# A planner that orders TensorE's work, single-bank PSUM tiles and merged loads in an attention-and-gate kernel

## The chip, the cores and the metric

The kernel runs on one core of one Trainium2 chip. The metric is the device time of one execution in microseconds (us). The kernel before takes 529.25 us, the median of 5 runs (528.02 to 530.52). Engines are named as in the profile: PE is TensorE (its weight loads are PEld), DVE is VectorE, ACT is ScalarE, POOL is GpSimd, SP is SyncE.

One more quantity is used throughout: **us of columns**. A matmul streams its columns; 512 of them start 215 ns apart when the clock is full. Counted from the shapes in the trace, all matmuls of the kernel stream 327 us of columns at full clock (at 215 ns for 512 columns it would be 330 us; all counts here are that 1% low). That is the least time that TensorE could need, and the change does not touch it. A few matmul records can be missing from a trace; the sum found is 314 us for the kernel before. By the weight loads that have no matmul beside them, about 4 us of what is missing lie before 220 us in the kernel before, and about 3 us in the changed kernel.

## The reference, cut to what matters

```python
def attention(q, k, v, w_phi):            # 8 batches, 8 heads, 576 rows, 64 wide
    def phi(x):
        proj = x @ w_phi                   # 64 -> 128 features
        proj = proj - max(abs(proj), axis=-1)
        return concat([exp(proj), exp(-proj)], axis=-1)
    qp, kp = phi(q), phi(k)
    kv, z = kp^T @ v, sum(kp, rows)
    return (qp @ kv) / (qp @ z + 1e-6)

def gate(x, w_proj, filter_fft, w_out):    # x: 8 x 576 x 512
    x1, x2, x3 = split(x @ w_proj, 3)
    conv = irfft(rfft(x2) * rfft(filter_fft))
    return (x1 * conv * x3) @ w_out

out = gate(attention(...))
```

The work falls into 16 attention units (one for half the heads of a batch) and 8 gate batches. A gate batch needs both attention units of its batch: the attention output is transposed (`xT`), folded on POOL (`G`), multiplied by the weights (`x2`), transformed (`fwd`), multiplied by the filter's spectrum (`spec`), transformed back (`inv`) and multiplied by the output weights (`fin`). The filter's spectrum and the trig tables for the transforms are computed once at the start; this is called the set-up here.

## The kernel before

First, steps are put in a fixed order by time numbers:

```python
TIMES = [0.00, 0.03, 0.06, 0.10, 0.16, 0.22, ...]       # the 18 steps of a unit
for t in range(NHALF):                                  # 16 attention units
    if t >= 2:
        order.append((t - 1.5, ld))                     # its loads
    for i in range(18):
        order.append((t + TIMES[i], run))
for b in range(NB):                                     # 8 gate batches
    for i, fn in enumerate(gs):
        order.append((2 * b + 2.2 + 2.0 * i / len(gs), fn))
order.sort(key=lambda x: x[0])
```

So one gate batch is spread over the two attention units that come after its own. Attention and gate run in lockstep.

Second, the projections go through two PSUM tiles of two banks each, and one reduce or exponential reads a whole tile:

```python
def proj(c, shape, name):
    return c.psum.tile(shape, FP32, name=name, tag="proj", bufs=2)

def pk(hp):
    pp = proj(c, [P, 2, 4, P], "Pk")
    # ... 4 matmuls of 256 columns ...
    nc.vector.tensor_reduce(out=mxk..., in_=pp, op=ALU.max, apply_absolute_value=True)
    nc.scalar.activation(s.Ekp[hp], pp, AF.Exp, scale=1.0)
    nc.scalar.activation(s.Ekm[hp], pp, AF.Exp, scale=-1.0)
    # the row maxima go into v: exp(-+max), then v times it, on POOL
    nc.gpsimd.tensor_tensor(out=v12[:, sg, :, 0:HD], in0=s.vs[...], in1=v12[:, sg, :, 64:65]..., op=ALU.mult)
```

Third, each unit issues 12 loads on POOL's queue (24 a batch); `q` comes in four pieces. Fourth, two small VectorE steps make the transposed maxima of `q`, and the output transpose is copied out in one contiguous copy:

```python
def mt():
    nc.vector.tensor_copy(M2[:, :, :, 0], mxq)
    nc.vector.tensor_tensor(out=M2[:, :, :, 1], in0=mxq, in1=M2[:, :, :, 0], op=ALU.subtract)
    # ... 5 transposes, copy to mT ...
```

## Time and profile before

| kernel before | value |
|---|---|
| time | 529.25 us (528.02 to 530.52) |
| PE busy | 387.4 us, 73% |
| POOL busy | 325.4 us, 62% |
| DVE busy | 297.9 us, 56% |
| ACT busy | 243.1 us, 46% |
| columns to stream | 327 us |

The first lines of the page of the kernel before: busy time per engine, then the busy tenths of two engines and of the granted TensorE clock in 40 equal slices of 13.2 us, then the engines of the chain that ended last.

```profile
PE 387.4 (73%) x3600; PEld 227.0 (43%) x3661; DVE 297.9 (56%) x512; ACT 243.1 (46%) x451; POOL 325.4 (62%) x454
...
PE   1134627696878779787878778877978698878796
...
POOL 9949996949566592759385674659294534344400
PEclk9999859798998999799989999799979989989999
...
POOL 39%; PE 20%; issue 18%; ACT 10%; DVE 9%; DMA 3%; POOLq 0%; DVEq 0%; ACTq 0%
```

No engine is full over the span. PE runs mostly at seven or eight tenths from a quarter of the way on; POOL is nearly full in the first quarter.

The waits view of the kernel before: the engine that stood idle and its instruction, what ended the wait, then the total in us, how often, and the longest.

```profile
POOL ks L349 <- PE ktp L375: 76.6, 11, 8.9
...
POOL v L409 <- ACT v L404: 29.2, 10, 4.1
...
PE acc L596 <- POOL G L242: 26.0, 8, 4.1
```

POOL stands 76.6 us at loads that wait for a buffer, and TensorE then waits 26.0 us for the fold `G` that POOL does late.

The windows view of the kernel before: busy us of each engine (and instructions) in four stretches, the mean clock, the DMA share and GB/s.

```profile
0.00:100.00 100.00, 39.26 (x373) 27.09 (x378) 60.84 (x132) 34.45 (x67) 88.11 (x132) 0.89 0.74 79
100.00:220.00 120.00, 97.52 (x896) 56.23 (x910) 66.44 (x106) 58.73 (x108) 79.50 (x110) 0.91 0.40 50
220.00:340.00 120.00, 97.16 (x908) 56.11 (x924) 67.08 (x111) 60.12 (x110) 76.32 (x106) 0.94 0.40 50
340.00:460.00 120.00, 98.27 (x966) 57.88 (x982) 66.30 (x108) 64.81 (x122) 65.16 (x89) 0.96 0.26 38
```

The first number after the length is PE, the third DVE, the fourth ACT, the fifth POOL. After 100 us the kernel is in a steady state: PE busy 97 of 120 us in every stretch.

Three groups of instructions of the kernel before (line, engine, operation, out<-in and shapes, count, busy us and mean ns of one, idle before it):

```profile
L409 POOL TENSOR_TENSOR v<-vs,v 128x512 bf16<-128x512 bf16 x64 | 66.2, 1061 | 29.3 <-ACT v L404 29.2
...
L427 DVE TENSOR_REDUCE mxk<-Pk 128x8 f32<-128x1024 f32 x32 | 38.9, 1217 | 8.1 <-PE Pk L421 7.9
L430 ACT ACTIVATE Ekp<-Pk 128x1024 bf16<-128x1024 f32 x32 | 32.8, 1024 | 19.3 <-DVE mxk L427 19.3
```

### The profile page before, as it was taken

Reading aid. Unit: us, or ns where it says so; the run is one execution under the profiler, and the core shown is the slowest. Engines: PE = TensorE matmul, PEld = TensorE weight load, DVE = VectorE, ACT = ScalarE, POOL = GpSimd, SP = SyncE. Lnnn points to the kernel's source line nnn. Section 1 sums busy time; section 2 is a strip of 40 time slices with the busy share of each in tenths; the row PEclk is TensorE's granted clock in tenths of the full one; section 3 lists DMA queues with packets and bytes.
Section 4 is the critical chain, followed back from the end, with each engine's and each line's share of the span. In section 5 each row is a group of like instructions: output and inputs, shape, how many; then the busy total and the mean of one; then the engine's idle time right before and its main releaser. Section 6 shows DMA issues by size and latency. Waiting matters only on the chain.

```text
span 527.5 us, 9126 instructions
## 1 busy us (share of the span) xinstructions
PE 387.4 (73%) x3600; PEld 227.0 (43%) x3661; DVE 297.9 (56%) x512; ACT 243.1 (46%) x451; POOL 325.4 (62%) x454
## 2 busy tenths in 40 slices
PE   1134627696878779787878778877978698878796
PEld 1023515253544546344544535344635455454443
DVE  2980774429462767439452947258551947385353
ACT  0345225383526552474337453466238443835240
POOL 9949996949566592759385674659294534344400
PEclk9999859798998999799989999799979989989999
DMA  7998615525261713525272525243372002000202
GB/s 70 84 202 77 56 18 52 45 24 47 24 127 9 66 22 66 73 24 46 24 134 25 46 24 110 27 47 23 64 94 25 0 1 91 1 1 1 90 1 90
DMA packets 71882, 27.03 MB, mean 51 GB/s; under 512 B 49120, under 2 KB 66720, under 8 KB 71840
## 3 DMA queue, kind: packets, MB, share of 16 engines
q0 software_dynamic: 66432, 16.89, 34.0%
q1 hardware_dynamic: 5408, 9.57, 5.0%
q8 instruction: 28, 0.46, 0.4%
q14 instruction: 14, 0.11, 0.1%
HBM read 33.75 MB, written 9.44 MB: 82 GB/s over the span
## 4 chain that ended last, share of the span: by engine, by line
POOL 39%; PE 20%; issue 18%; ACT 10%; DVE 9%; DMA 3%; POOLq 0%; DVEq 0%; ACTq 0%
POOL v L409 6%; PE acc L596 5%; POOL qs L353 5%; POOL vt L471 3%; PE acc L623 3%; POOL eox L237 3%; POOL kt L344 3%; POOL eox L238 3%; POOL G L242 3%; POOL G L243 3%; ACT Eqm L505 3%; DMA wproj<-in_moe_w_proj_dram 2%; POOL vt L344 2%; ACT Eqp L500 2%; DVE P L615 2%
## 5 line engine op out<-in xcount | busy, mean ns | idle before, releaser
L409 POOL TENSOR_TENSOR v<-vs,v 128x512 bf16<-128x512 bf16 x64 | 66.2, 1061 | 29.3 <-ACT v L404 29.2
L623 PE MATMUL acc<-xT,wproj 128*128 128x64 bf16 (+1 forms) x496 | 75.9, 289 | 0.5
L596 PE MATMUL acc<-wproj,G 128*128 128x512 bf16 x126 | 45.2, 487 | 27.3 <-POOL G L242 26.0
L349 POOL DMA_DIRECT2D ks<-in_k_dram x16 | 12.5, 781 | 78.0 <-PE ktp L375 76.6
L441 DVE TENSOR_REDUCE mxq<-Qn 128x8 f32<-128x1024 f32 x32 | 38.9, 1216 | 32.5 <-PE Qn L439 32.5
L353 POOL DMA_DIRECT2D qs<-in_q_dram x64 | 48.8, 785 | 4.0 <-PE xtp L557 2.7
L598 ACT CAST x2n<-acc 128x512 bf16<-128x512 f32 x40 | 23.5, 589 | 51.1 <-PE acc L596 46.2
L674 DVE TENSOR_TENSOR yT<-acc,ts 128x512 bf16<-128x512 f32 x32 | 22.2, 692 | 43.2 <-PE acc L664 43.2
L500 ACT ACTIVATE Eqp<-Pq 128x1024 bf16<-128x1024 f32 x32 | 33.2, 1037 | 27.6 <-PE Pq L495 23.6
L505 ACT ACTIVATE Eqm<-Pq 128x1024 bf16<-128x1024 f32 x32 | 32.7, 1022 | 23.5 <-PE Pq L502 21.5
L427 DVE TENSOR_REDUCE mxk<-Pk 128x8 f32<-128x1024 f32 x32 | 38.9, 1217 | 8.1 <-PE Pk L421 7.9
L430 ACT ACTIVATE Ekp<-Pk 128x1024 bf16<-128x1024 f32 x32 | 32.8, 1024 | 19.3 <-DVE mxk L427 19.3
L543 DVE RECIPROCAL r<-NE 128x10 f32<-128x10 f32 x32 | 6.9, 216 | 61.4 <-PE NE L539 61.4
L664 PE MATMUL acc<-IV,Y 128*128 128x512 bf16 (+1 forms) x254 | 41.2, 285 | 0.4
L623 PEld LDWEIGHTS <-wproj 128*128 128x128 bf16 x512 | 32.6, 99 | 17.5 <-issue 1.7
L690 PE MATMUL acc<-wout,yT 128*128 128x512 bf16 x147 | 39.5, 379 | 0.7
L633 ACT CAST x1s<-acc 128x512 bf16<-128x512 f32 x32 | 18.9, 590 | 44.2 <-PE acc L623 40.7
L439 PE MATMUL Qn<-wpp,qT 128*128 128x256 bf16 x128 | 22.9, 310 | 19.3 <-DVE qT L391 16.5
L596 PEld LDWEIGHTS <-G 128*128 128x128 bf16 x128 | 13.5, 116 | 50.0 <-POOL G L242 29.8
L694 ACT COPY o<-acc 128x512 f32<-128x512 f32 x16 | 9.4, 586 | 53.9 <-PE acc L690 41.3
L569 POOL COPY xT<-xT 128x2 bf16<-128x2 bf16 x16 | 3.5, 221 | 47.8 <-DVE xT L567 47.8
L431 ACT ACTIVATE Ekm<-Pk 128x1024 bf16<-128x1024 f32 x32 | 32.8, 1025 | 0.0
(180 smaller groups left out, 1091.9 us busy)
## 6 DMA issues: line engine op xcount, KB each, us to landing
out_dram<-o SPq DMA_DIRECT2D x32, 256.0 KB, 2.2
ks<-in_k_dram POOLq DMA_DIRECT2D x16, 256.0 KB, 4.4
qs<-in_q_dram POOLq DMA_DIRECT2D x64, 64.0 KB, 3.4
vs<-in_v_dram POOLq DMA_DIRECT2D x16, 256.0 KB, 4.2
wproj<-in_moe_w_proj_dram POOLq DMA_DIRECT2D x4, 384.0 KB, 10.0
out_dram<-o SPq DMA_DIRECT2D x8, 128.0 KB, 3.0
kt<-in_k_dram POOLq DMA_DIRECT2D x32, 16.0 KB, 3.4
qt<-in_q_dram POOLq DMA_DIRECT2D x32, 16.0 KB, 2.2
```

The costliest lines, as they stand in the source:

```text
L353: nc.gpsimd.dma_start(out=s.qs[:, ci, :, :], in_=q[b, h0:h0 + 4, ci * P:(ci + 1) * P, :].rearrange("h p d -> p h d"))
L409: nc.gpsimd.tensor_tensor(out=v12[:, sg, :, 0:HD], in0=s.vs[:, 2 * hp:2 * hp + 2, :, :].rearrange("p j c d -> p (j c) d"), in1=v12[:, sg, ...
L427: nc.vector.tensor_reduce(out=s.mxk[:, 8 * hp:8 * hp + 8].rearrange("p (j c) -> p j c", j=2), in_=pp, axis=AX.X, op=ALU.max, apply_absolut ...
L430: nc.scalar.activation(s.Ekp[hp], pp, AF.Exp, bias=0.0, scale=1.0)
L431: nc.scalar.activation(s.Ekm[hp], pp, AF.Exp, bias=0.0, scale=-1.0)
L441: nc.vector.tensor_reduce(out=mxq[:, 0:4, 2 * hp:2 * hp + 2], in_=pp, axis=AX.X, op=ALU.max, apply_absolute_value=True)
L500: nc.scalar.activation(s.Eqp[hp], pp, AF.Exp, bias=0.0, scale=1.0)
L505: nc.scalar.activation(s.Eqm[hp], pp, AF.Exp, bias=0.0, scale=-1.0)
L596: nc.tensor.matmul(acc, lhsT=lhsT, rhs=c.wproj[:, kt, 512:1024], start=(kt == 0), stop=(kt == 3))
L623: nc.tensor.matmul(acc, lhsT=c.wproj[:, kt, base + m * P:base + (m + 1) * P], rhs=xT[:, kt, s0:s1], start=(kt == 0), stop=(kt == 3))
L664: nc.tensor.matmul(acc, lhsT=Y, rhs=c.IV[:, kt, s0:s1], start=(kt == 0), stop=(kt == 5))
L690: nc.tensor.matmul(acc, lhsT=yT[:, kt, ci * P:(ci + 1) * P], rhs=c.wout[:, kt, :], start=(kt == 0), stop=(kt == 3))
```

## The change

The intent is to keep TensorE fed. The fixed time numbers go; every step becomes an object with its TensorE time, its needs and the engine work that it causes, and a planner simulates the engines while the kernel is being built. It takes, at each point, the first step that can start without delay, attention before gate. Attention thereby runs ahead of the gate, and gate steps fill TensorE's holes. Alongside: the two-bank PSUM tiles become single banks, with a reduce and two exponentials for each; loads are merged into 11 issues a batch; `spec` is cut in four and the tails in two; `xT` is written in another row order, by a strided copy of 512 columns and a short one.

```diff
-TIMES = [0.00, 0.03, 0.06, 0.10, 0.16, 0.22, ...]
+class Planner:
+    # free time of each engine, events, PSUM slots
+    def run(self, streams, window):
+        while any(streams):
+            best = None
+            for r, strm in enumerate(streams):
+                for k, st in enumerate(strm[:window(r)]):
+                    t = self.start_of(st)
+                    late = max(0, t - self.free["PE"] - 40)
+                    if best is None or late < best[0]:
+                        best = (late, strm, k)
+                    ...                       # stop at the first with late == 0
+            st = best[1].pop(best[2]); self.emit(st); out.append(st)

-def proj(c, shape, name):
-    return c.psum.tile(shape, FP32, name=name, tag="proj", bufs=2)
+def halves(c, shape, name):
+    return [c.psum.tile(shape, FP32, name=name, tag="proj", bufs=4) for _ in range(2)]

-            nc.scalar.activation(s.Ekp[hp], pp, AF.Exp, bias=0.0, scale=1.0)
+            for (i, j) in enumerate((1, 0)):
+                nc.vector.tensor_reduce(out=mx[:, 4 * i:4 * i + 4], in_=pp[i], ...)
+                nc.scalar.activation(Ep[:, j], pp[j], AF.Exp, bias=0.0, scale=1.0)
+                nc.scalar.activation(Em[:, j], pp[j], AF.Exp, bias=0.0, scale=-1.0)

-    s.ks = c.stage.tile([P, 4, 4, HD], BF16, name="ks", tag="ks", bufs=3)
+            setattr(s, nm, c.stage.tile([P, 2, 4, 4, HD], BF16, name=nm, tag=nm, bufs=2))
 ...
-            nc.vector.tensor_copy(xT[:, kt, 0:SEQ], tp[:, 0:SEQ])
+            nc.vector.tensor_copy(xTs[b][:, kt, 0:512].rearrange("d (p c) -> d p c", c=4),
+                                  tp[:, 0:512].rearrange("d (c p) -> d p c", c=4))
+            nc.vector.tensor_copy(xTs[b][:, kt, 512:SEQ], tp[:, 512:SEQ])
 ...
-    for _, fn in order:
-        fn()
+    pl.free.update({"PE": 8000, "ACT": 14000, "DVE": 14000, "POOL": 8000, "DMA": 8000})
+    order = pl.run([loads, attn, gate], (1, 26, 12).__getitem__)
+    for st in order:
+        st.fn()
```

## The prediction

> **What bounds it now.** No engine is full. In each steady batch (58.1 us from one batch's first x2 matmul to the next, 158.3 to 390.7 us, windows view) PE is busy 46.7 us, POOL 37.9, DVE 32.6, ACT 28.8. The matmuls stream 327 us of columns at full clock in all (counted from the shapes; 40.3 us a batch; a 512-column matmul starts every 215 ns). The rest is order: POOL stands about 8.9 us a batch at a k load that waits for the k transposes (77 us in all, waits view), issues 24 loads a batch (16.8 us), and only then folds; PE waits 3.6-4.1 us a batch for G from the fold (26 us). After that wait the granted clock is 0.50-0.56 for some 6 us (425 ns per 512 columns), about 3 us lost a batch. The Trainium skill ("TensorE: Matmul & The Clock Gate", Part 1) describes just this halving after an idle window; the trace agrees. The start is worse: the first x2 matmul begins at 100.9 us; POOL is nearly full until there, PE at 20-60%.
>
> **What changes.** (1) A planner orders all steps so that PE always has something ready; attention runs ahead of the gate. In the built order the last attention matmul comes after about 220 us of the 327 us of columns; the last 107 are pure gate. (2) PSUM tiles of two banks become single banks. (3) Loads per batch: 24 issues become 11; q in 1 KB runs. (4) spec is cut in four, tails in two.
>
> **Cost by engine, from durations in the trace.**
> - POOL a batch: folds 11 + v 8.5 + vt 3.3 + issues 11 x 0.75 = 31, less overlap 4% = 30 us (was 38). All eight, with 10 us of spectrum folds and 15 us of set-up and weight issues: about 263 us.
> - DVE: a 512 reduce, interpolated between 415 ns (256) and 1217 ns (1024), is 0.68 us; 64 more of each kind add 9.5 us each. Smaller xn steps add 11. The xT copy becomes strided: 0.44 us contiguous becomes about 0.8 us in two pieces (I take the uncompressed rate of the 683 ns 512 copy): +11. In all 298 to about 335.
> - ACT: 1024 exps of 1.02 us become two of 0.60: +20; ten table loads of 1.28 us at the start instead of two: +10; in all about 285.
> - PE: the same columns.
>
> **Sum.** Phase A, until attention ends: POOL 263, DVE 257, ACT 241, PE 235 us. All close, so none will be filled: plus 12 us of start and 15 of friction, about 290 us. Phase B: 107 us of gate, which keeps PE near full (at 500-520 us PE is busy 19.9 of 20 at clock 1.00): about 115. End: 5. Together about 412 us.
>
> **Predicted 412 us**, 388 to 450; faster by over 2% 0.97, within 0.02, slower 0.01.
>
> **Right if the profile shows:** POOL total 255-275 us busy, DVE 320-350, ACT 270-300; PE share over 80%; first x2 at 80-92 us; PE windows after about 295 us at 9 tenths with clock near 1.0 and POOL empty; half-clock stretches after G waits gone; POOL's wait for k transposes below 25 us; packets down from 66,432 by about 25,000. In phase A the chain of waits runs over POOL, ACT and DVE.
>
> **Wrong if:** in-order queues block each other in phase A (ACT behind table loads, POOL behind a load whose buffer isn't free), pushing it above 320 us; or the start's load queue holds attention of batch 0 up; or bubbles between spec, inv and fin in phase B exceed 4 us a batch. Better than said if phase A's engines reach 95%.

## The result, and the profile after

The changed kernel takes 457.3 us (median of 9 runs, 455.76 to 458.88), the kernel before 529.93 us in the same rounds (median of 16). The ratio is 0.8632, with a 95% interval of 0.8615 to 0.8648. A ratio here is the mean time of one kernel's fast runs over the mean time of the other's fast runs of the same rounds, so it is not quite the ratio of the medians that are quoted. Executions over 1.5% slower than the fastest of the same kernel are left out of the means. The kernel is faster by 14%, about 45 us less than the predicted gain, and outside the predicted range of 388 to 450 us.

The same lines of the page of the changed kernel (40 slices of 11.4 us).

```profile
PE 378.7 (83%) x3679; PEld 236.3 (52%) x3725; DVE 329.8 (73%) x703; ACT 261.5 (58%) x604; POOL 265.3 (58%) x352
...
PE   3326877579688769799798989999999999999995
...
POOL 9946998979966996954964647164542345000000
PEclk9659868698899969989899999999999999999999
...
PE 45%; POOL 20%; DVE 14%; ACT 8%; issue 8%; DMA 4%; DVEq 0%; POOLq 0%; ACTq 0%
```

PE's row has two halves. In the first 16 slices (some 180 us) it hardly differs from the kernel before: mostly five to eight tenths, with the clock dropping again and again. From the 23rd slice on (some 250 us) it stands at eight or nine tenths, mostly nine, with the clock at full.

The waits view of the changed kernel:

```profile
POOL v L608 <- ACT v L604: 30.3, 9, 5.1
...
POOL ks L499 <- PE kTp L560: 4.6, 3, 2.7
...
PE KV L722 <- POOL v L608: 14.2, 10, 4.9
PE Pk L589 <- DVE mxq L625: 10.0, 9, 5.0
```

POOL's wait for the `k` buffers fell from 76.6 to 4.6 us, and TensorE's 26.0 us wait for the fold `G` is gone from the list. What TensorE waits for now is `v` from POOL and the row maxima from DVE.

The windows view of the changed kernel, in the same stretches as before:

```profile
0.00:100.00 100.00, 58.09 (x595) 41.16 (x598) 71.45 (x192) 62.22 (x136) 84.87 (x126) 0.80 0.75 95
100.00:220.00 120.00, 98.95 (x1162) 68.77 (x1173) 95.76 (x207) 81.89 (x208) 95.52 (x126) 0.93 0.52 66
220.00:340.00 120.00, 113.46 (x1192) 72.39 (x1208) 100.62 (x205) 78.72 (x193) 66.35 (x83) 0.99 0.15 31
340.00:460.00 120.00, 108.24 (x735) 53.94 (x748) 61.99 (x103) 38.71 (x71) 18.54 (x19) 0.99 0.15 50
```

Between 100 and 220 us PE is busy 98.95 us, against 97.52 before: nothing gained, although DVE went from 66 to 96 us and ACT from 59 to 82. From 220 us on PE is busy 113 of 120 us, and POOL only 66. (The last stretch ends with the span at 454.6 us.)

Busy time hides half clock, so the columns that were streamed say it better. This table is counted from the matmuls in the traces:

| us of columns streamed by | 100 us | 220 us | 340 us | last attention matmul (`NE`) |
|---|---|---|---|---|
| kernel before | 23 | 102 | 182 | 491 us |
| changed kernel | 34 | 112 | 214 | 342 us |

By 220 us the change has brought only 10 us of columns (9 with the missing records put back, 115 against 106). All the rest of its 72 us comes later, when attention is ahead and the gate work that has piled up keeps TensorE full.

The groups of the changed kernel that answer to those shown of before:

```profile
L608 POOL TENSOR_TENSOR v<-vs,v 128x512 bf16<-128x512 bf16 x64 | 69.1, 1109 | 30.4 <-ACT v L604 30.3
...
L598 DVE TENSOR_REDUCE mxk<-Pk 128x4 f32<-128x512 f32 x64 | 42.3, 680 | 7.5 <-PE Pk L589 4.6
L602 ACT ACTIVATE Ekm<-Pk 128x512 bf16<-128x512 f32 x64 | 39.9, 626 | 0.0
```

The reduce of half the size takes 680 ns, as the prediction had interpolated; two of them cost more than one of 1217 ns.

### The profile page after: what moved, and what is told of

It reads as the page before. It is cut to its first block, busy times and chain, and to the rows that moved or that the text cites. A ratio compares the mean times of both kernels' runs of the same rounds, so it can differ in the third digit from the quotient of the medians.

```text
span 454.6 us, 9516 instructions
## 1 busy us (share of the span) xinstructions
PE 378.7 (83%) x3679; PEld 236.3 (52%) x3725; DVE 329.8 (73%) x703; ACT 261.5 (58%) x604; POOL 265.3 (58%) x352
## 3 DMA queue, kind: packets, MB, share of 16 engines
q0 software_dynamic: 40256, 16.88, 31.3%
## 4 chain that ended last, share of the span: by engine, by line
PE 45%; POOL 20%; DVE 14%; ACT 8%; issue 8%; DMA 4%; DVEq 0%; POOLq 0%; ACTq 0%
PE acc L931 10%; PE acc L972 8%; POOL v L608 6%; PE acc L896 5%; PE acc L998 5%; PE NE L745 3%; POOL vt L672 3%; DVE mxq L625 2%; DMA out_dram<-o 2%; DMA vt<-in_v_dram 2%; POOL vt L494 2%; ACT Eqp L697 2%; DVE mxk L598 1%; ACT Eqm L709 1%; PE KV L722 1%
## 5 line engine op out<-in xcount | busy, mean ns | idle before, releaser
L697 ACT ACTIVATE Eqp<-Pq 128x512 bf16<-128x512 f32 x64 | 36.4, 628 | 40.3 <-PE Pq L691 40.0
L601 ACT ACTIVATE Ekp<-Pk 128x512 bf16<-128x512 f32 x64 | 39.5, 622 | 31.9 <-PE Pk L589 28.0
L598 DVE TENSOR_REDUCE mxk<-Pk 128x4 f32<-128x512 f32 x64 | 42.3, 680 | 7.5 <-PE Pk L589 4.6
L625 DVE TENSOR_REDUCE mxq<-Qn 128x4 f32<-128x512 f32 x64 | 40.9, 680 | 2.2 <-PE Qn L621 2.2
L602 ACT ACTIVATE Ekm<-Pk 128x512 bf16<-128x512 f32 x64 | 39.9, 626 | 0.0
L709 ACT ACTIVATE Eqm<-Pq 128x512 bf16<-128x512 f32 x64 | 36.7, 648 | 2.8 <-PE Pq L706 2.6
L589 PE MATMUL Pk<-wpp,kT 128*128 128x256 bf16 x128 | 23.8, 292 | 13.8 <-DVE mxq L625 10.0
L722 PE MATMUL KV<-v,Ekp 128*128 128x65 bf16 x256 | 21.1, 208 | 11.9 <-POOL v L608 11.7
L672 POOL TENSOR_TENSOR vt<-vt,emt 128x130 bf16<-128x130 bf16 x64 | 23.9, 401 | 11.4 <-ACT emt L668 11.4
L751 DVE TENSOR_TENSOR xn<-NE,rc 128x320 bf16<-128x320 f32 x64 | 29.0, 483 | 0.3
## 6 DMA issues: line engine op xcount, KB each, us to landing
wproj<-in_moe_w_proj_dram POOLq DMA_DIRECT2D x4, 384.0 KB, 10.6
```

The lines of the kernel that those rows point to most:

```text
L598: nc.vector.tensor_reduce(out=mx[:, 4 * i:4 * i + 4], in_=pp[i], axis=AX.X, op=ALU.max, apply_absolute_value=True)
L601: nc.scalar.activation(Ep[:, j], pp[j], AF.Exp, bias=0.0, scale=1.0)
L602: nc.scalar.activation(Em[:, j], pp[j], AF.Exp, bias=0.0, scale=-1.0)
L625: nc.vector.tensor_reduce(out=mxq[:, 0:4, 2 * hp + j], in_=pp[j], axis=AX.X, op=ALU.max, apply_absolute_value=True)
L672: nc.gpsimd.tensor_tensor(out=s.vt12[:, sg, hp], in0=sg_of().vt[:, g, hp], in1=emt[:, sg].to_broadcast([P, 2, 65]), op=ALU.mult)
L697: nc.scalar.activation(s.Eqp[hp][:, j].rearrange("f (c p) -> f c p", c=4), pp[j], AF.Exp, bias=0.0, scale=1.0)
```

## The experiments

Eighteen kernels were run, each against the kernel before on the same chip. The texts call the theories by letters. The first two were A, that POOL's throughput bounds the first half, and S, that a late start does. Later ones were Q (POOL's load queue at the start), C (TensorE's half clock), M (what the planner doesn't know becomes a stall that is never made up), D (VectorE), O (the order holds gate work back) and P (set-up work fills the first 100 us). Differences "against the changed kernel" are between medians and its 457.3 us. All diffs are against the changed kernel and cut to what matters. The columns of ww_late come from a slow run.

| run | median us | ratio to before, 95% interval | columns by 100 / 220 / 340 us |
|---|---|---|---|
| (changed kernel) | 457.3 | 0.8632 (0.8615 to 0.8648) | 34 / 112 / 214 |
| old_order | 531.5 | 1.0026 (1.0004 to 1.0047) | 30 / 111 / 192 |
| psum_pair | 490.4 | 0.9240 (0.9208 to 0.9273) | 31 / 97 / 190 |
| split_loads | 456.4 | 0.8622 (0.8563 to 0.8680) | 34 / 118 / 223 |
| dup_early | 475.6 | 0.8985 (0.8965 to 0.9005) | 32 / 101 / 203 |
| dup_late | 468.2 | 0.8846 (0.8822 to 0.8869) | 35 / 113 / 210 |
| dup_early_told | 470.0 | 0.8839 (0.8803 to 0.8875) | 34 / 111 / 208 |
| ffold_dve | 458.4 | 0.8658 (0.8633 to 0.8683) | 35 / 115 / 219 |
| trig_first | 459.9 | 0.8688 (0.8662 to 0.8713) | 33 / 113 / 216 |
| ww_late | 470.4 | 0.8803 (0.8753 to 0.8852) | 33 / 103 / 203 |
| start_late | 470.8 | 0.8899 (0.8867 to 0.8930) | 28 / 103 / 207 |
| plan_cal | 459.0 | 0.8648 (0.8631 to 0.8665) | 35 / 116 / 219 |
| warm | 467.1 | 0.8795 (0.8765 to 0.8825) | 34 / 106 / 209 (without the dummies) |
| mx_act | 454.4 | 0.8547 (0.8520 to 0.8573) | 34 / 115 / 218 |
| dve_light | 451.0 | 0.8509 (0.8482 to 0.8536) | 33 / 118 / 227 |
| start_light | 454.5 | 0.8578 (0.8530 to 0.8625) | 33 / 113 / 223 |
| gate_first | 494.2 | 0.9325 (0.9295 to 0.9355) | 34 / 125 / 214 |
| no_setup (wrong result) | 449.3 | 0.8491 (0.8466 to 0.8515) | 40 / 115 / 214 |
| no_setup_start (wrong result) | 440.1 | 0.8308 (0.8292 to 0.8323) | 43 / 116 / 222 |

### Which part of the change brings the gain

**old_order**: every other part of the change, but the old kernel's fixed times in place of the planner.

```diff
-    order = pl.run([loads, attn, gate], (1, 26, 12).__getitem__)
+    timed = [(old time of the step, st) for st in loads + attn + gate]   # units at t, gate at 2b+2.2...
+    order = [st for _, st in sorted(timed, key=lambda x: x[0])]
```

> All parts of the change but the planner: the new steps (loads per batch, single PSUM banks, cut spec and tails) in the old kernel's fixed time order. If the order is the main gain, 495 to 525 us; if the smaller loads and tiles are, 455 to 480 us.

It took 531.5 us, as long as the kernel before, and longer than either expectation. Without the planner the other parts together bring nothing. One by one, only the single banks (psum_pair) and the merged loads (split_loads) were tried; the cut `spec` and tails and the new row order of `xT` were not.

**psum_pair**: the planner, but the projections in two PSUM tiles of two banks again. Each half is still read by its own instruction; only the release is by pair.

```diff
-    return [c.psum.tile(shape, FP32, name=name, tag="proj", bufs=4) for _ in range(2)]
+    t = c.psum.tile([P, 2, 512], FP32, name=name, tag="proj", bufs=2)
+    return [t[:, j, :]... for j in range(2)]
```

> The changed kernel with the four single PSUM banks put back into two tiles of two banks. The planner counts pairs anyway, so the plan is the same. If finer PSUM tiles matter: 465 to 480; if not: 455 to 461.

It took 490.4 us, 33 us more, and more than the text had expected. So with the planner up to 33 of the 72 us hang on the single banks; old_order has them too and gains nothing. Not all of the 33 us need be owed to the release by pair. In the kept trace the two steps on `M` got stuck at 41 us, beside `v` and `vt` products of POOL, for 7.7 and 3.3 us, and the first `KV` came at 54.4 us instead of 41.9; what this is worth was not measured.

**split_loads**: 18 load issues a batch instead of 11 for batches 1 to 7; the planner knows of them.

```diff
-    halves = [(0, 1), (1, 2)] if b == 0 else [(0, 2)]
+    halves = [(0, 1), (1, 2)]
```

> The changed kernel with 18 load issues a batch instead of 11 for batches 1 to 7: 7 x 7 x 0.65 = 32 us more POOL work, about 23 us of it before 200 us. By the slope that the doubled v work showed (about 1 early, 0.6 late): 20 to 30 us longer, 477 to 487. If only work between the k max and KV counts and the issues fall into idle time: under 8 us longer.

It took 456.4 us: no change. The windows view of split_loads and then of the changed kernel, from 60 to 220 us:

```profile
60.00:220.00 160.00, 125.65 (x1399) 82.96 (x1396) 126.53 (x260) 104.20 (x257) 154.73 (x208) 0.91 0.51 62
```

```profile
60.00:220.00 160.00, 128.21 (x1472) 90.44 (x1488) 123.36 (x267) 102.38 (x258) 132.00 (x178) 0.90 0.56 69
```

POOL is busy 154.73 of 160 us instead of 132.00, and the kernel is as fast. An engine that can take 23 us more in the very stretch that loses the time is not what limits it by its throughput. Theory A falls in this form, and the merged loads, by themselves, bring nothing here. One rival is left: the smaller loads may also have helped attention by landing piece by piece, and this run does not separate the two. The chain of waits says where POOL still counts. From 42 to 220 us, 89 of its 178 us lie on POOL in the changed kernel, and 48 in split_loads, where DVE has 68; from 220 to 340 us none of it lies on POOL in either, and PE leads with 71 and 63 us.

### POOL's work on the way to KV

**dup_early** and **dup_late** do the `v` products of head pair 0 twice, in units 0 to 7 or in units 8 to 15; the second overwrites the first with the same values. The planner isn't told.

```diff
-            for sg in range(2):
+            for sg in ((0, 1, 0, 1) if hp == 0 and t < 8 else (0, 1)):      # dup_late: t >= 8
                 nc.gpsimd.tensor_tensor(out=v12[:, sg, :, 0:HD]...
```

> The changed kernel with the two v multiplications of the first head pair done twice in units 0 to 7 (same values again): 8 x 2 x 1.06 = 17 us more work on POOL, all of it in about the first 190 us. Theory A (the first 200 us are paced by POOL, busy 175 of 200 us there, the rest by PE): 10 to 17 us longer than the changed kernel, so 467 to 474. Rival B (the time is lost to PE's order and half clock, POOL is only a neighbour): under 5 us longer. Rival C (PE paces everything): no change.

> The same doubling in units 8 to 15 instead: again 17 us more on POOL, but nearly all after 180 us, where POOL idles half the time and PE is 94 to 99% busy. Theory A: 0 to 3 us longer (457 to 460). If POOL paced the attention to its end, as the prediction had it: 10 us or more longer.

dup_early added some 17 us of POOL work (15.8 by the busy time) and cost 18.3 us, a little more than theory A's 10 to 17. dup_late cost 10.9 us, where theory A had expected almost nothing: most of the loss falls at 220 to 240 us, before the piled-up gate work keeps TensorE full (PE is busy 11.2 us there, 17.3 in the changed kernel). In the same 20 us two steps on `M` took 2.2 and 3.8 us in dup_late, so a part of the cost may be what VectorE loses beside POOL (see ffold_dve below) and not the length of the chain.

**dup_early_told** is dup_early with the planner's cost for these products doubled as well.

```diff
-                  ("POOL", pool(512), ("em" + h,), "v1_" + h),
+                  ("POOL", pool(512) * (2 if hp == 0 and t < 8 else 1), ("em" + h,), "v1_" + h),
```

> The same 17 us of extra GpSimd work as in dup_early (v products of head pair 0 twice in units 0 to 7), but the planner's own cost for them is doubled too, so it can order around them. Its plan then ends 3.9 us later than the changed kernel's plan. Theory M (what the plan doesn't know becomes a TensorE stall, one for one, that is never made up; what it knows it can hide): 458 to 464 us, so most of dup_early's 18.3 us come back. Rival theory A (GpSimd's throughput in the first half is the bound): 472 to 478 us, as dup_early.

It took 470.0 us, between the two expectations: knowing the cost brings back 6 of the 18 us by the medians (8 by the ratios). Theory M is right in a small part only. Read with split_loads, these runs suggest that it matters where POOL's work stands: 23 us of load issues off the chain cost nothing, and 17 us on the chain from the row maxima through `v` to `KV` cost 11 to 18.

**ffold_dve** takes the filter's fold (10.6 us) off POOL and gives it to DVE.

```diff
-            fold(c, nc.gpsimd, st["fT"], st["G"], kt, 2, "f")
+            fold(c, nc.vector, st["fT"], st["G"], kt, 2, "f")
```

> The changed kernel with the fold of the filter spectrum on DVE instead of POOL: 10.6 us of POOL work between 50 and 61 us go away and some 6 us of DVE work come. Theory A: 6 to 10 us shorter (447 to 451). Rival B: under 3 us.

It took 458.4 us: no gain. One of the moved steps met the `v` products. The tile view of ffold_dve, with durations in ns as shortest, median and longest:

```profile
L371 DVE TENSOR_TENSOR Gf<-eof x2: 458/4698/8937, 40.6 to 51.7; 128x580 bf16<-128x580 bf16 x2
```

The same step took 0.46 us once and 8.94 us the other time, while POOL ran 14 `v` and `vt` products back to back. So this run says little about POOL's load; it shows what DVE loses beside POOL.

### The start

The first `KV` matmul comes at 41.9 us. POOL issues loads until 40.8 us, held up from 22.6 us on, and ACT's exponentials for the tails wait behind trig table loads until 34.6 us. The next runs take these holds away.

**trig_first** computes the trig tables ahead of everything (table loads fall from 11 to 4).

```diff
+    for g in trig_groups(c):
+        g()
     make_consts(c, w_phi)
 ...
-    for g in trig_groups(c):
-        g()
```

> The changed kernel with the trigonometric tables emitted before the constants and loads: the built order then has 4 activation table loads instead of 11 at the start. Theory S (the start is late by ACT's table switching and DVE's table arithmetic; the changed kernel's first KV ends at 47 us): 7 to 12 us shorter. Theory A in its strict form (POOL, held at the load queue to 40.8 us by the weights' landing, paces the start too): under 3 us shorter.

459.9 us: no gain. The trace shows that POOL's first `v` product still starts at 41.9 us.

**ww_late** loads the gate's weights after batch 1's loads and unit 1's `v` products.

```diff
-    loads += weight_steps(c, moe_w_proj, moe_filter_fft, moe_w_out)
-    for b in range(1, NB):
+    wf, ww = weight_steps(c, moe_w_proj, moe_filter_fft, moe_w_out)
+    ww.need = ["a1.v12_1"]
+    loads += [wf] + load_steps(c, 1, q, k, v, stages) + [ww]
+    for b in range(2, NB):
```

> The changed kernel with the projection and output weights loaded after batch 1's loads and after unit 1's v products. Theory Q (POOL's in-order queue stands at the load queue behind the weights' landing until 40.8 us, so the first v product, ready to start at about 23 us, starts then): first KV ends before 42 instead of 47 us and the time falls 4 to 10 us. If the first units are held by ACT and DVE instead: within 3 us.

470.4 us, slower. Two of its four runs, the profiled one among them, count as slow, so the ratio rests on two runs (464.6 and 468.7 us). POOL's first `v` product came earlier, at 32.1 us, but the first `KV` did not: in the trace, which is of a slow run, two DVE steps on `M` got stuck for 5.5 and 2.9 us beside POOL's work. This run took away one hold of two and doesn't decide.

**start_late** takes both away: trig is built after unit 0's `KV`, batch 1's loads wait for unit 0's `v` products, and the weights for unit 1's.

```diff
-    for g in trig_groups(c):
-        g()
+    gate.insert(4, Step("trig", trig, 0, ["a0.KV1"], [("DVE", 15000, (), "trigd"), ("ACT", 9000, (), "triga")]))
 ...
+    for st in l1: st.need = ["a0.v12_1"]          # loads of batch 1
+    ww.need = ["a1.v12_1"]
```

> Trig is built after unit 0's KV, the loads of batch 1 wait for unit 0's v products and the weights for unit 1's, so neither GpSimd's queue nor ScalarE's table loads stand before the first KV (47 us in the changed kernel). Both theories: first KV at 18 to 26 us. Theory S (the late start is handed on to the end): 432 to 446 us. Rival (the early pace is set by when gate work comes, and the start only shifts attention): 452 to 464 us, first x2 of batch 0 not before 105 us.

470.8 us, slower by 13 us and slower than both expectations, though the first `KV` matmul now came at 24.6 us. The windows view from 40 to 120 us, of the changed kernel and then of start_late:

```profile
40.00:120.00 80.00, 56.75 (x628) 41.06 (x630) 52.13 (x123) 45.38 (x115) 76.04 (x102) 0.83 0.61 70
```

```profile
40.00:120.00 80.00, 42.17 (x477) 28.74 (x477) 72.52 (x145) 42.71 (x108) 63.60 (x84) 0.73 0.69 87
```

The set-up moved to where it fills DVE (72.5 of 80 us) and holds up unit 1 instead of unit 0; the first `x2` matmul came at 118 us instead of 108. Theory S falls in this form: the set-up must be done before any gate work, and putting it later costs more.

### The planner's numbers, the clock, VectorE

**plan_cal** gives the planner the starts and costs that the trace showed.

```diff
-    pl.free.update({"PE": 8000, "ACT": 14000, "DVE": 14000, "POOL": 8000, "DMA": 8000})
+    pl.free.update({"PE": 8000, "ACT": 30000, "DVE": 26000, "POOL": 11700, "DMA": 11700})
-                 [("DVE", dve2(576), (), "xT" + h)]
+                 [("DVE", 780, (), "xT" + h)]          # and xn 820, rc 200, 9.5 us more for one load
```

> Only the planner's numbers change: the start of ACT, DVE, POOL and the hold-up of the load queue as the trace showed them, and the costs of the xT copy (780 instead of 375 ns) and of xn and its reciprocal. Its own plan then ends at 434 us (415 before), and the first unit's last KV is planned for 50 us (36 before; 47 measured). Theory M in its strong form (a truer plan is a better order): 440 to 452 us. Rival (the truer plan only foretells the loss, the order has no better use for TensorE in the first 200 us): 454 to 461 us.

459.0 us: no change. A truer plan foretells more of the loss (its own end moves from 415 to 434 us) and finds no better order.

**warm** puts twelve dummy matmuls of 256 columns before each `KV` in units 0 to 9.

```diff
+            if t < 10:
+                flat = acc.rearrange("p a b x -> p (a b x)")
+                for _ in range(12):
+                    nc.tensor.matmul(flat[:, 0:256], lhsT=c.ident, rhs=c.wpp, start=True, stop=True)
```

> Twelve dummy matmuls of 256 columns (1.3 us at full clock) before each KV in units 0 to 9, to hold TensorE's clock up over the wait for v. 63 us of the changed kernel's span are at half clock. If half clock drives the early loss (theory C): half-clock time below 40 us and 440 to 452 us. If it follows from the waits: half-clock time may fall, time 456 to 466 us.

467.1 us, slower by 10 us, with half-clock time down from 63 to 36 us. The page "TensorE: Matmul & The Clock Gate" of the Trainium skill, Part 1, says that the clock falls to half when the engine idles and comes back after a few us of work. The traces agree: the dummies do hold the clock up. This run alone does not price half clock, since the 240 dummies are themselves about 26 us of columns in TensorE's queue. The four runs of dup_late say more: their mean granted clocks lie between 0.921 and 0.959, which is 18 us of full clock over 466 us, and their times within 0.8 us (467.7 to 468.4). In the profiled runs dup_late has no half clock before 40 us and the changed kernel has 20 us of it, and both have streamed 8 us of columns by then. So half clock that falls into waits costs nothing here; that it costs nothing anywhere is not shown.

**mx_act** replaces the two steps on `M` by one copy on ACT and leaves the residual zero. The outputs are right.

```diff
-        nc.vector.tensor_copy(M2[:, :, :, 0], mxq)
-        nc.vector.tensor_tensor(out=M2[:, :, :, 1], in0=mxq, in1=M2[:, :, :, 0], op=ALU.subtract)
+        nc.scalar.copy(M2[:, :, :, 0], mxq)
```

> The two tiny VectorE steps on M are replaced by one copy on ScalarE, and the residual is left zero (the result may be a little wrong, on purpose). In the changed kernel these two took 19.3 us for a sum of minima of 6.8. If VectorE steps that get stuck beside GpSimd carry the early loss: 445 to 452 us. If they are a symptom: 454 to 459 us; and the excess moves to the spec products.

454.4 us, better by 2.9 us, or by 4.5 us if the ratios are compared ((0.8632 - 0.8547) x 530). That lies in the range for a symptom, and some of the excess moved as foreseen: the `spec` products on `P` took 40.2 us in sum instead of 37.2. The groups of the changed kernel show what the two steps cost, where their shortest took 0.19 and 0.23 us:

```profile
L637 DVE CAST M<-mxq 128x20 bf16<-128x20 f32 x16 | 10.0, 626 | 0.1
L638 DVE TENSOR_TENSOR M<-mxq,M 128x20 bf16<-128x20 f32 x16 | 9.3, 583 | 0.2
```

On ACT no copy gets stuck; the tile view of mx_act has shortest, median and longest close together:

```profile
L637 ACT CAST M<-mxq x16: 262/282/382, 37.5 to 314.6; 128x20 bf16<-128x20 f32 x16
```

The page "SBUF — State Buffer" of the Trainium skill, in "SBUF: two separate sides", describes an exclusive lock between GpSimd and those VectorE instructions that use the shared pair of ports (in a two-port mode, or with two inputs in SBUF), which blocks the loser fully. The traces agree with it: the copy at 120.4 us in the changed kernel took 3.43 us while POOL ran `G`, four `vt` products and `G` again.

**dve_light** is mx_act with all `xT` copies on ACT, which the planner knows.

```diff
-            nc.vector.tensor_copy(xTs[b][:, kt, 0:512]..., tp[:, 0:512]...)
-            nc.vector.tensor_copy(xTs[b][:, kt, 512:SEQ], tp[:, 512:SEQ])
+            nc.scalar.copy(xTs[b][:, kt, 0:512]..., tp[:, 0:512]...)
+            nc.scalar.copy(xTs[b][:, kt, 512:SEQ], tp[:, 512:SEQ])
```

> mx_act, and all xT copies on ScalarE, which the planner knows: about 27 us less on VectorE, as much more on ScalarE. Theory D (VectorE is what attention waits for before 220 us): 440 to 450 us. If not: 452 to 458 us, as mx_act (0.8547 of the kernel before).

451.0 us, the fastest correct kernel, and its ratio interval lies wholly below the changed kernel's. DVE falls from 329.8 to 295.8 us:

```profile
PE 374.7 (84%) x3725; PEld 233.1 (52%) x3725; DVE 295.8 (66%) x607; ACT 282.0 (63%) x684; POOL 266.4 (60%) x352
```

The gain is 6.3 us, a little less than theory D had asked for. VectorE is a part of the early loss, and a small one. Against mx_act the `xT` copies bring 3.4 us by the medians and 2 by the ratios, whose intervals overlap, so their own share is not clear.

**start_light** is start_late and dve_light together.

```diff
+    # the edits of start_late and of dve_light
```

> start_late and dve_light together. If S and D both hold: 425 to 440 us; if neither: 450 to 462 us; if only one, that one's time.

454.5 us: between the two, slower than dve_light alone. It is 16 us faster than start_late. So lightening VectorE is worth 16 us where the set-up stands late and 6 where it does not, and such single gains do not simply add.

### The order, and the set-up

**gate_first**: the planner prefers a gate step to an attention step when both are ready.

```diff
-    order = pl.run([loads, attn, gate], (1, 26, 12).__getitem__)
+    order = pl.run([loads, gate, attn], (1, 12, 26).__getitem__)
```

> The planner prefers a gate step to an attention step where both are ready (the two streams and their windows change places). Its own plan ends at 443 us (415 for the changed kernel). If the order held back gate work that TensorE could have used without harm to attention (theory O): under 450 us and batch 1's x2 before 160 us. If attention's pace is what counts: batch 1's x2 before 160 us, but attention ends later than 390 us, and 480 to 500 us in all.

494.2 us. Batch 1's last `x2` copy came at 151 us instead of 224, so gate work was indeed being held back; but columns by 220 us rose only from 112 (115 with the missing records) to 125, and attention ended at 454 us instead of 342. The windows view of gate_first:

```profile
220.00:340.00 120.00, 100.75 (x1038) 62.94 (x1035) 80.08 (x172) 59.54 (x143) 59.08 (x78) 0.94 0.33 51
340.00:460.00 120.00, 102.82 (x1041) 63.33 (x1040) 78.57 (x170) 65.99 (x157) 51.27 (x65) 0.94 0.09 31
```

This kernel is in lockstep like the kernel before, with a gate batch about every 54 us (58 before). PE is busy 101 to 103 of 120 us in it, for good. From 220 to 340 us it streams 89 us of columns, the changed kernel 102 (about 106 with its missing records).

**no_setup** sets the trig tables and the filter's spectrum to zero instead of computing them, and **no_setup_start** also moves the loads as in start_late. Both give a wrong result.

```diff
-    for g in trig_groups(c):
-        g()
+    for each of FM, FR, RM, RR, IV, H1, H2: nc.vector.memset(tile, 0.0)
-    gate = spectrum_steps(c)
+    gate = [Step("f.H", lambda: None, 0, ["filt"])]
```

> The trig tables and the filter's spectrum are memset to zero instead of computed (a wrong result, on purpose); loads, weights, attention and gate are as in the changed kernel. It takes away about 14 us of VectorE, 20 of ScalarE with its table loads, 10.6 of GpSimd's folds and 5 of TensorE's columns. Theory P (the first 100 us are set-up and attention alone, and attention can't fill TensorE): first x2 of batch 0 at 70 to 85 us instead of 108, and 425 to 442 us. If the loss is owed to attention's pace alone: 447 to 453 us (less the 5 us of columns).

> no_setup, and batch 1's loads after unit 0's v products, the weights after unit 1's (a wrong result, on purpose). With neither set-up nor a blocked queue the first KV should come at 18 to 28 us. Theory P: 412 to 430 us, x2 of batch 0 at 60 to 75 us. If attention's pace alone: 440 to 453 us.

no_setup took 449.3 us, 8.0 us less, of which 5 us are the spectrum's own columns. no_setup_start took 440.1 us, 17.2 us less, so 12 us beyond those columns. Batch 0's first `x2` came at 75 and 63 us instead of 108, and still only 115 and 116 us of columns had been streamed by 220 us. The first `x2` came as early as theory P had said, but both times lie in the ranges for its rival, attention's pace. What is left of theory P is a part: set-up and start together are worth about 12 of the 45 us that were missed.

## Why the prediction was right or wrong

**Right: what bound the kernel before, and what the planner does about it.** POOL's wait for the `k` buffers fell to 4.6 us (predicted below 25), the waits for `G` went, software packets fell from 66,432 to 40,256 (predicted about 25,000 fewer), POOL is busy 265.3 us (255 to 275), DVE 329.8 us (320 to 350), PE 83% (over 80%). In the last stretch PE is at nine tenths or more with the clock at full. That stretch, after attention's last matmul at 342 us, took 113 us to the end of the span at 454.6 us; the prediction had about 115 and an end of 5.

**Wrong: "Phase A, until attention ends ... about 290 us".** This is the step that failed. Phase A ended at 342 us (the last `NE` matmul; the last transpose came at 364 us), 52 us later. It was mis-sized because it was built as the largest engine sum (POOL, 263 us) plus 27 us, as if the 220 us of columns that lie in phase A could be streamed anywhere in it. Spread over 290 us they would have made 167 us of columns by 220 us (220 x 220/290). The runs showed 112 (115 with the missing records), and 97 to 125 (no more than 118 but for gate_first) in every kernel, dummies left out. TensorE then streamed 102 us of columns between 220 and 340 us and was busy 113 of 120 us there, while POOL was busy only 66: this part of phase A is bound by TensorE, not by POOL, DVE or ACT. The "friction" of 15 us was thus the term that was far too small: phase A lay 79 us above POOL's 263, and 12 of these had been set down for the start. Two of the prediction's own warnings came true, a phase A above 320 us and a load queue that holds up the first batch; but the runs that took the queue's hold away (start_late, and no_setup_start for 12 us at most) show that it isn't the larger part. Two stages with different limits cannot be sized by one sum over both.

**What the early stage lacks.** Before the first `x2` there is no gate work at all. In the kernels that compute the set-up it came at 85 us at the earliest (old_order), and in gate_first at 101 us, with 34 us of columns streamed by 100 us. From 100 to 220 us there is gate work, but in the one other order that was tried it had to be bought with attention: gate_first takes it early, streams 10 to 13 us more by 220 us, and then stays in lockstep at 89 us of columns in 120 for the rest. The changed kernel holds it back, lets attention run ahead, and streams 102 in the next 120 us and nearly everything after. The gain is made by a stock of ready gate work, and building the stock is what the first 220 us are spent on. The prediction counted the full benefit of the stock (107 us of gate at the end) and didn't charge for building it. gate_first and the columns support this reading; that no third order does better than both was not shown.

**Smaller misses.** The first `x2` came at 108 us, not at 80 to 92, and later than in the kernel before: there the first `x2` matmul ran at 92.1 us, and the 100.9 us of the prediction are the start of the first copy out of `x2`. ACT was busy 261.5 us, not 270 to 300: the prediction added mean durations, but successive exponentials of 512 start 0.48 us apart at 0.58 to 0.62 us each, so they overlap. Half clock did not go away; it fell from 73 to 63 us and moved into the first 240 us. POOL was not empty after 295 us, since attention still ran. The chain of waits named POOL (20%), DVE (14%) and ACT (8%) beside PE, as said, but PE leads with 45%: in phase A the chain lies mostly on POOL up to 220 us, and on PE after.

**What is settled of the 45 us, and what is open.** Of single causes in the early stage, set-up and start are worth about 12 us beyond their columns, and VectorE's load with its stuck steps 6 us; they were not measured together without the other changes, so adding them is an estimate, 18 us, and start_light warns against adding. By runs, the following are not the cause in the form tested: POOL's throughput (split_loads), half clock (dup_late, warm), the planner's false numbers (plan_cal) and gate work first (gate_first). No run took work off POOL without putting it in VectorE's way (ffold_dve), so what POOL's steps on the chain are worth, 89 of its 178 us from 42 to 220 us, was tried only by adding to them. What else keeps attention at its pace is open. It is sensitive to the time from the row maxima through `v` to `KV` (dup_early) and to how finely PSUM is released (psum_pair, up to 33 us), which points to a loop of waits through buffers rather than to a full engine; that is argued and not shown. A run with four instead of three buffers for the exponentials would have tested it; with four of each the kernel does not fit into SBUF.

## What to carry to other kernels

Don't size a phase by the largest engine sum when one stream of work makes the input of the other: ask, for each stretch, what is ready for the bottleneck engine then, and count the columns that it can stream until that time. Running a producer ahead makes a stock that keeps the bottleneck full later, but the stock must be paid for at the start. Before moving work off an engine, add work to it in the suspected stretch where it hurts no chain: if the time doesn't move (POOL, 23 us more in 160), its throughput was likely not the limit.

## What the Trainium skill lacked or had wrong

- "SBUF — State Buffer", "SBUF: two separate sides", says that the loser of the lock waits for the whole instruction of the other. The runs show waits over several: a VectorE copy of 20 columns took 3.43 us (0.19 at its shortest) while GpSimd instructions of 0.4 to 1.2 us followed one another, and a fold step in ffold_dve took 8.94 us (0.46 at its shortest) across about a dozen of them. The page doesn't say that a busy GpSimd can hold VectorE off that long.
- "ScalarE: Activation LUTs", "What ACT_TABLE_LOAD costs", gives 1283 ns for the load and about 1380 ns more for a drain at each switch. The load is 1283 ns in the trace too, but the switch costs no more than that: at the start of the changed kernel one exponential ends at 17.47 us, the load begins at 17.49 and the next activation at 18.78 us.
- The same section says that activations back to back overlap by about 93 ns. The exponentials of 512 columns overlap by about 120 ns here, starting 0.48 us apart at 0.60 us each.
- No page has anything on how to size a kernel in which one engine-bound stream feeds another; the number that was missed here is the 112 us of columns in the first 220 us.
